# Loading the second expert matrix in whole rows, with the combine weights prepared among the experts' matmuls

## The chip, the cores and the metric

The kernel runs on one core of a Trainium2 chip. The metric is the device time of one execution in microseconds; the time of a kernel is the median of its runs.

## The reference

Three layers follow each other on 4,608 tokens (8 batches of 576) of width 512.

```python
# 1. attention in chunks of 64 tokens, 8 heads of 64
attn = softmax(q_c @ k_c.T / sqrt(64)); x = attn @ v_c
# 2. a feed-forward layer, 512 -> 2048 -> 512
h = np.maximum(x @ w_in, 0.0); x = h * h @ w_out
# 3. soft mixture of 8 experts with 4 slots each
logits = x @ phi                                  # 4608 x 32
slot_input = softmax(logits, over tokens).T @ x   # 32 x 512
for e in range(8):
    slot_out[e] = np.maximum(slot_input[e] @ w1[e], 0.0) @ w2[e]
out = softmax(logits, over slots) @ slot_out      # 4608 x 512
```

w1 is 8 x 512 x 1024 and w2 is 8 x 1024 x 512, all float32: 16.8 MB each. The output is 9.44 MB.

## The kernel before

The tokens go through in 36 tiles of 128 (64 tokens of two batches each), gathered in blocks of three. For most of the time TensorE makes the hidden layer of a block (`moe_h`, L727), turns it (L761) and keeps it in buffers G; w_out is never applied to tokens, only to slot sums. A running softmax over tokens (`soft(b)`) adds the block's G, weighted, to the slot sums (L928).

The last block is the one the change touches. Its `soft` runs a chain: logits Ls (L854), the sum over quarters (L864), their maximum (L874 to L876, nm), the exponential dts on ScalarE (ACT, L877), its transposes (L917), the weights dd (L919), 24 matmul pieces over G (L928), the sum acc on VectorE (DVE, L939). Then `slot_turn` transposes acc (L807), `slot_rows_of` multiplies by w_out (L817), each copied out by `halves` (L801 on ACT, L802 on DVE, both from one PSUM bank), and `slot_inputs` (L827, L831) makes the experts' input siT. Between these, `c_two` prepares combine weights for four groups of four tiles: transposes on TensorE (L1047), two ACT copies a group (L1055, L1060) and a GpSimd subtraction (L1061).

Then come the experts. Their weights arrive in 64 units of 512 KB, 32 of w1 and then 32 of w2. `load_units` sends a unit as soon as two halves of 512 columns are free, from a list `free` that `give` and `release` fill: attention buffers of the last tiles, the buffers of w_in (wi), the last G after L928, those of w_out (wo) after L817, and places of units that have been used. A unit in one buffer goes in one DMA (L985 for w1, L994 for w2), one in two half places in two (L988, L999). `kept_tags` names eight buffers that end as homes of combine weights cT or of the turned hidden layer hT; `give` sets the first `(C_CHAIN + 1) // 2` of them aside empty, the others hold a unit first. All DMAs go through SyncE (SP) in the order that a planner sets by a simulated time; TensorE's order is that of the source, and so is that of all engines in the early part of the kernel.

w1's matmuls (L1468) go by group of four experts (g), row block (kk) and half; then the hidden layer (L1441, L1442) is turned (`hidden_T`, L1451). w2's matmuls (L1584) run twice, for output columns 0 to 255 (ch = 0) and 256 to 511 (ch = 1); a unit of w2 is 512 rows by 256 columns. After each half, `slot_rows` and `slot_parts` (L1492, L1497 to L1501) make the slot outputs s4. The output of half 0 (`out_group`: matmuls L1553, copies L1555 on DVE and L1557 on ACT) runs among the matmuls of half 1, and so do the other five groups of combine weights (`c_group`); the output of half 1 runs at the end. An output group of four tiles is one DMA (L1568); a single tile at the border of two batch pairs goes as two DMAs of 64 partitions by 1 KB (L1574, 16 in all).

## Time and profile before

| | us |
|---|---|
| median of 3 runs | 772.77 |
| lowest to highest run | 772.29 to 775.29 |
| the profiled execution, device time | 774.87 |
| its span on the core | 773.1 |

| engine | busy us | share of the span |
|---|---|---|
| PE (TensorE matmul) | 711.1 | 92% |
| ACT (ScalarE) | 457.3 | 59% |
| DVE (VectorE) | 428.1 | 55% |
| POOL (GpSimd) | 161.9 | 21% |

The span is the stretch between the first and the last instruction of the profiled execution; the device time holds a little more. A share of busy time is a mean over stages with different limits, so the rows below look at the last 100 us by themselves. In a window's row stand its length, the busy time of PE, PEld (weight loads), DVE, ACT and POOL with their counts of instructions, the granted TensorE clock (1.00 is 2.4 GHz), the mean busy share of the 16 DMA engines (it can read over 1) and the bytes that they moved per second. Matmuls in float32 show as two pieces each.

### The profile page before, as it was taken

Reading aid. Unit: us, or ns where it says so; the run is one execution under the profiler, and the core shown is the slowest. Engines: PE = TensorE matmul, PEld = TensorE weight load, DVE = VectorE, ACT = ScalarE, POOL = GpSimd, SP = SyncE. Lnnn points to the kernel's source line nnn. Section 1 sums busy time; section 2 is a strip of 40 time slices with the busy share of each in tenths; the row PEclk is TensorE's granted clock in tenths of the full one; section 3 lists DMA queues with packets and bytes.
Section 4 is the critical chain, followed back from the end, with each engine's and each line's share of the span. In section 5 each row is a group of like instructions: output and inputs, shape, how many; then the busy total and the mean of one; then the engine's idle time right before and its main releaser. Section 6 shows DMA issues by size and latency. Waiting matters only on the chain.

```text
span 773.1 us, 16704 instructions
## 1 busy us (share of the span) xinstructions
PE 711.1 (92%) x6612; PEld 457.7 (59%) x6612; DVE 428.1 (55%) x908; ACT 457.3 (59%) x951; POOL 161.9 (21%) x209
## 2 busy tenths in 40 slices
PE   5788999898999999999999999999999999969790
PEld 3677776665666566565665656666666565524350
DVE  4789996267756656567665566566656201012160
ACT  3668787664656666666676566566766555531150
POOL 3222221131222312223132231322223100030000
PEclk9799999999999999999999999999999999999995
DMA  7897933233455534455544655454556523759998
GB/s 158 215 257 180 218 123 124 72 66 83 98 117 103 103 76 97 91 103 104 101 97 83 103 101 112 75 103 89 99 88 171 159 69 112 277 178 354 347 355 255
DMA packets 242589, 110.47 MB, mean 143 GB/s; under 512 B 201808, under 2 KB 235600, under 8 KB 242512
## 3 DMA queue, kind: packets, MB, share of 16 engines
q1 hardware_dynamic: 242512, 109.41, 57.7%
q8 instruction: 52, 0.85, 0.5%
q14 instruction: 25, 0.20, 0.1%
HBM read 78.71 MB, written 9.44 MB: 114 GB/s over the span
## 4 chain that ended last, share of the span: by engine, by line
PE 71%; DMA 10%; DVE 9%; ACT 4%; issue 1%; POOL 1%; SPq 1%; DVEq 0%; POOLq 0%; ACTq 0%
PE hps L727 41%; PE gT L761 7%; PE misc L928 4%; PE L L778 4%; DMA unit<-in_moe_w_dram 3%; PE ehps L1468 2%; DVE qk L276 2%; DMA qkT<-qk 2%; DMA qkv<-in_k_dram 2%; DMA qkv<-in_q_dram 1%; PE misc L332 1%; DMA qkv<-in_v_dram 1%; DVE stage L281 1%; PE misc L498 1%; DVE qk L275 1%
## 5 line engine op out<-in xcount | busy, mean ns | idle before, releaser
L727 PE MATMUL hps<-xb,wi 128*128 128x384 f16 (+2 forms) x2400 | 409.2, 321 | 0.3
L727 PEld LDWEIGHTS <-wi 128*128 128x128 f16 x2400 | 225.1, 98 | 139.9 <-issue 18.3
L742 ACT ACTIVATE g<-hps,inv_w 128x384 f32<-128x384 f32 (+1 forms) x200 | 112.6, 563 | 113.0 <-PE hps L727 110.8
L182 DVE TENSOR_REDUCE am<-qkv 128x1 bf16<-128x512 f32 x90 | 61.9, 687 | 89.9 <-DMA qkv<-in_v_dram 45.8
L188 ACT ACTIVATE G<-gT 128x384 f32<-128x384 f32 (+1 forms) x200 | 94.1, 471 | 17.9 <-PE gT L761 15.3
L761 PE MATMUL gT<-ident,g 128*128 128x128 f32 x576 | 98.3, 278 | 4.6 <-ACT G L188 3.7
L749 ACT ACTIVATE g<-g 128x384 f32<-128x384 f32 (+2 forms) x188 | 96.9, 515 | 1.5
L761 PEld LDWEIGHTS gT<-ident,g 128*128 128x128 f32 x576 | 73.0, 144 | 29.6 <-ACT g L749 7.1
L420 POOL TENSOR_SCALAR vbd<-qkv,as 64x512 f16<-64x512 f32 x54 | 37.2, 689 | 87.5 <-PE misc L500 71.8
L471 POOL TENSOR_TENSOR ex<-ex,rs 128x512 f32<-128x512 f32 x27 | 29.3, 1083 | 122.4 <-DVE rs L468 110.3
L410 DVE SCALAR_TENSOR_TENSOR qk<-qkv,as,qk 128x512 f16<-128x512 f32 x54 | 39.7, 762 | 20.4 <-ACT qk L405 19.8
L425 DVE SCALAR_TENSOR_TENSOR vbd<-qkv,as,vbd 64x512 f16<-64x512 f32 x54 | 44.7, 828 | 0.7
L778 PE MATMUL L<-g,wp 128*32 128x384 f32 x384 | 41.7, 498 | 0.0
L405 ACT ACTIVATE qk<-qkv,as 128x512 f16<-128x512 f32 x54 | 36.8, 717 | 7.9 <-DVE as L215 7.9
L484 POOL TENSOR_TENSOR p<-ex,p 128x512 f16<-128x512 f32 x27 | 36.2, 1341 | 16.5 <-ACT p L481 15.9
L481 ACT ACTIVATE p<-ex 128x512 f16<-128x512 f32 x27 | 17.0, 629 | 34.6 <-POOL ex L471 34.4
L928 PE MATMUL misc<-G,dd 128*32 128x512 f32 x288 | 35.1, 622 | 0.5 <-DVE rs__8963 L936 0.5
L435 DVE COPY qbd<-qkT 64x1024 f16<-64x1024 f16 x54 | 23.3, 431 | 18.3 <-DMA qkT<-qk 17.5
L510 DVE SCALAR_TENSOR_TENSOR xb<-misc,xb 128x512 f16<-128x512 f32 x27 | 18.5, 685 | 26.5 <-ACT xb L504 26.2
L223 POOL TENSOR_SCALAR iv_all<-ai 128x1 f32<-128x1 f32 x27 | 7.4, 273 | 108.5 <-DVE ai L218 107.6
L854 DVE TENSOR_TENSOR Ls<-L,iv_all 128x384 f32<-128x384 f32 x12 | 6.7, 557 | 41.5 <-PE L L778 41.5
L461 ACT ACTIVATE ex<-ex,es 128x512 f32<-128x512 f32 x27 | 19.4, 718 | 17.0 <-DVE ex L455 16.9
(156 smaller groups left out, 1018.9 us busy)
## 6 DMA issues: line engine op xcount, KB each, us to landing
unit<-in_moe_w_dram SPq DMA_DIRECT2D x34, 512.0 KB, 4.5
unit<-in_moe_w_dram SPq DMA_DIRECT2D x60, 256.0 KB, 5.9
qkv<-in_q_dram SPq DMA_DIRECT2D x72, 128.0 KB, 3.3
qkv<-in_k_dram SPq DMA_DIRECT2D x72, 128.0 KB, 3.5
qkv<-in_v_dram SPq DMA_DIRECT2D x72, 128.0 KB, 3.3
stage<-in_moe_w_in_dram SPq DMA_DIRECT2D x16, 512.0 KB, 5.3
stage<-in_moe_w_out_dram SPq DMA_DIRECT2D x16, 512.0 KB, 5.8
out_dram<-o SPq DMA_DIRECT2D x14, 512.0 KB, 6.3
```

What stands on the lines that cost most here:

```text
L182: dve.tensor_reduce(out=am, in_=src, axis=AX.X, op=ALU.max, apply_absolute_value=True)
L188: act.activation(out=out, in_=in_, func=ACTF.Copy)
L405: act.activation(out=qk16[:, 2 * a], in_=flat[:, a], func=ACTF.Copy, scale=v["s"][:, a : a + 1])
L410: dve.scalar_tensor_tensor(out=qk16[:, 2 * a + 1], in0=flat[:, a], scalar=v["s"][:, a : a + 1], in1=qk16[:, 2 * a], op0=ALU.mult, op1=ALU. ...
L420: pool.tensor_scalar(out=dst[0], in0=vin, scalar1=v["s"][pr, 2:3], scalar2=1.0, op0=ALU.mult, op1=ALU.mult,)
L425: dve.scalar_tensor_tensor(out=dst[1], in0=vin, scalar=v["s"][pr, 2:3], in1=dst[0], op0=ALU.mult, op1=ALU.subtract,)
L727: pe.matmul(hp, wi[f][:, wl, kt], xb[:, xl, kt], start=(nm == 0), stop=(nm == 3 * KT - 1))
L742: act.activation(out=g, in_=hp, func=ACTF.Relu, scale=sc)
L749: act.activation(out=g, in_=g, func=ACTF.Square)
L761: pe.transpose(gt_ps[b, f][:, j], g[:, j * P : (j + 1) * P], ident)
L778: pe.matmul(L_ps[g0][NS * x : NS * x + NS, :n], wp[:, QF * q + x], g[:, x, :n], start=(q == 0), stop=(q == NQ - 1), tile_position=(0, NS * x),
L928: pe.matmul(y[NS * g : NS * g + NS], dd[:, j], G_q[b, g][:, j], start=(j == 0), stop=(j == n - 1), tile_position=(0, NS * g), skip_group_c ...
```

## The change

- **C_CHAIN** goes from 4 to 0. `c_two` then does nothing in the last block's chain, and no kept buffer is set aside empty, so the first two hold a unit each. All nine groups of combine weights go through `c_group`: three among w1's matmuls (the condition on C_EARLY, unchanged, now holds), six among w2's.
- **`slot_turn` and `slot_rows_of`** work in two column halves, each in a PSUM bank of its own; ACT copies the first, DVE the second. The matmuls of `slot_rows_of` become twice as many with half the columns.
- **From the last block on**, ACT and DVE too run in source order.
- **w2 in whole rows**: 20 of its 32 units ("rows": experts 0 to 3 whole, g = 0, and the first quarter of experts 4 to 7, g = 1) hold 256 whole rows of one expert, two rows to a partition, 4 KB in one run (two runs of 2 KB where the home is split). Their matmuls serve both column halves at once, in two PSUM accumulators. The other 12 ("part") hold 128 rows of four experts in 256 columns, half 0 first, then half 1. `hidden_T` takes its columns with a stride of two to fit.
- **The output** is cut anew: groups of four tiles of the first two batch pairs by column halves (half 0 among and after the last matmuls, half 1 at the very end); between them pairs of tiles with all 512 columns, and the single tiles two by two, in four DMAs of 256 KB.

Of the last hunks of the diff only what is added and what stays is shown.

```diff
--- before.py
+++ after.py
@@ -31,7 +31,7 @@
-C_CHAIN = 4
+C_CHAIN = 0
...
@@ -796,30 +796,31 @@
         for r in (32, 96):
             dve.memset(second[r : r + 32], -1.0)
 
-    def halves(out, in_):
-        n = in_.shape[-1] // 2
-        act.activation(out=out[:, :n], in_=in_[:, :n], func=ACTF.Copy)
-        dve.tensor_copy(out[:, n:], in_[:, n:])
+    def half_out(h, out, in_):
+        copy(("act", "dve")[h], out[:, h * DM // 2 : (h + 1) * DM // 2], in_)
 
     def slot_turn():
-        ps = misc()
-        for c in range(QF):
-            pe.transpose(ps[:, c * P : (c + 1) * P], acc[:, c * P : (c + 1) * P], ident)
         fin["yz"] = yz = big.tile([P, 2, DM], F32, tag="g1", name="yz")
-        yT = yz[:, 0]
-        halves(yT, ps)
+        for h in range(2):
+            ps = misc()[:, : DM // 2]
+            for x in range(QF // 2):
+                c = h * QF // 2 + x
+                pe.transpose(ps[:, x * P : (x + 1) * P], acc[:, c * P : (c + 1) * P], ident)
+            half_out(h, yz[:, 0], ps)
 
     def slot_rows_of():
-        ps = misc()
         yT = fin["yz"][:, 0].rearrange("p (c g s) -> p c g s", c=QF, s=NS)
-        for c in range(QF):
-            for g in range(NQ):
-                pe.matmul(
-                    ps[NS * g : NS * g + NS], yT[:, c, g], wo[QF * g + c],
-                    start=(c == 0), stop=(c == QF - 1), tile_position=(0, NS * g),
-                    skip_group_check=True,
-                )
-        halves(fin["yz"][:, 1], ps)
+        for h in range(2):
+            ps = misc()[:, : DM // 2]
+            for c in range(QF):
+                for g in range(NQ):
+                    pe.matmul(
+                        ps[NS * g : NS * g + NS], yT[:, c, g],
+                        wo[QF * g + c][:, h * DM // 2 : (h + 1) * DM // 2],
+                        start=(c == 0), stop=(c == QF - 1), tile_position=(0, NS * g),
+                        skip_group_check=True,
+                    )
+            half_out(h, fin["yz"][:, 1], ps)
 
     def slot_inputs():
         sip = misc()
@@ -849,6 +850,10 @@
     def soft(b):
         s0, n = blocks[NB if b == 1 else b]
         last = s0 + n == NT
+        if last:
+            ctx.enter_context(
+                tc.manual_schedule(engines={mybir.EngineType.Activation, mybir.EngineType.DVE})
+            )
         L, iv = L_ps.pop(b), iv2_all[:, s0 : s0 + n]
         Ls = big.tile([P, 4, P], F32, tag="Ls", name="Ls")[:, :n]
         dve.tensor_tensor(
@@ -955,12 +960,17 @@
...
 
     DH = DM // NCH
-    RT = 1024 // DH
-    units = [(0, 0, 4 * g + e, kk) for g in range(2) for kk in range(KT) for e in range(4)]
+    SPLIT = FT // 4
+    units = [("w1", 4 * g + e, kk) for g in range(2) for kk in range(KT) for e in range(4)]
     units += [
-        (1, ch, 4 * g + e, kk)
-        for ch in range(NCH) for g in range(2) for kk in range(FT // RT) for e in range(4)
+        ("rows", 4 * g + e, m)
+        for g in range(2) for m in range((SPLIT if g else FT) // 2) for e in range(4)
     ]
+    units += [("part", ch, ft) for ch in range(NCH) for ft in range(SPLIT, FT)]
+    def w2_rows(e, m):
+        return w2[e, 2 * P * m : 2 * P * (m + 1)].rearrange("(p t) d -> p t d", t=2)
 
     out_tags = (f"qkv{NT % 2}", f"qkv{(NT - 1) % 2}", f"G{idle_G[0]}")
     kept_tags = [f"{x}{y % 2}" for y in (NT - 1, NT) for x in ("qk16", "qkT", "qbd", "vbd")]
@@ -975,30 +985,28 @@
...
             home[u] = (a, b)
+            if u[0] == "w1":
+                _, e, kk = u
+                src = w1[e, kk * P : (kk + 1) * P, :].rearrange("p (h d) -> p h d", h=2)
+            elif u[0] == "rows":
+                src = w2_rows(*u[1:])
             else:
+                _, ch, ft = u
+                m = ft // 2
+                src = w2[4:, 2 * P * m : 2 * P * (m + 1), ch * DH : (ch + 1) * DH].rearrange(
+                    "e (p t) d -> p t e d", t=2
+                )[:, ft % 2]
+            n = src.shape[1] // 2
+            if whole_home:
+                to = a[0][:, a[1] : a[1] + 1024].rearrange("p (t d) -> p t d", t=2 * n)
+                sp.dma_start(out=to, in_=src)
+            else:
+                for h, (t, o, _) in enumerate((a, b)):
+                    to = t[:, o : o + 512].rearrange("p (t d) -> p t d", t=n)
+                    sp.dma_start(out=to, in_=src[:, h * n : (h + 1) * n])
 
     def freed(pool_, tag, n):
         t = pool_.tile([P, n], F32, tag=tag, name="unit", **({} if pool_ is big else {"bufs": 1}))
@@ -1447,8 +1455,9 @@
         for h in range(2):
             htp = ps2.tile([P, FT // 2, P], F32, tag=f"ht{h}", name="htp")
             for ft in range(FT // 2):
-                f0 = (h * FT // 2 + ft) * P
-                pe.transpose(htp[:, ft], hs[:, f0 : f0 + P], ident)
+                m, t = divmod(h * FT // 2 + ft, 2)
+                rows = hs[:, 2 * P * m : 2 * P * (m + 1)].rearrange("p (x t) -> p t x", t=2)
...
@@ -1505,114 +1514,119 @@
...
+    def out_buffer():
+        tags = [t for _, _, t in free]
+        for tag in tags:
+            if not todo and 512 * tags.count(tag) == size_of[tag] >= 1024:
+                free[:] = [x for x in free if x[2] != tag]
+                break
+        else:
+            tag = out_ring.pop(0)
+        out_ring.append(tag)
+        return big.tile([P, 1024], F32, tag=tag, name="o")
+    out_ring = list(out_tags)
+    banks = ("eh00", "eh01", "eh10", "eh11", "ht0")
+    bank = [0]
+    by_batch = out.rearrange("(b s) d -> s b d", s=S)
+    def out_group(parts, chs):
+        n, w = len(parts), len(chs) * DH
+        flat = out_buffer()
+        items = [(i, c, ch) for i, c in parts for ch in chs]
+        for x0 in range(0, len(items), 2):
+            ops = ps2.tile([P, 2, DH], F32, tag=banks[bank[0] % 5], name="ops")
+            for x, (i, c, ch) in enumerate(items[x0 : x0 + 2]):
+                rows = cT[i // 8][:, i % 8 + (c or 0)]
+                pe.matmul(ops[:, x], rows, s4_h[ch], start=True, stop=True)
+            dst = flat[:, x0 * DH : (x0 + 2) * DH].rearrange("p (x d) -> p x d", x=2)
+            if bank[0] % 2:
+                dve.tensor_copy(dst, ops)
+            else:
+                act.activation(out=dst, in_=ops, func=ACTF.Copy)
+            bank[0] += 1
+        o = flat[:, : n * w].rearrange("p (t d) -> p t d", t=n)
+        cols = slice(chs[0] * DH, chs[0] * DH + w)
+        bp, ci = divmod(parts[0][0], CPB)
+        if parts[0][1] is not None:
+            r0 = (2 * bp + parts[0][1]) * S + ci * CH
+            sp.dma_start(
+                out=out[r0 : r0 + n * P, cols].rearrange("(t p) d -> p t d", p=P), in_=o
+            )
+        else:
+            s0, (bq, cj) = ci * CH, divmod(parts[-1][0], CPB)
+            assert n == 2 and ci == cj
+            for c in range(2):
+                to = by_batch[s0 : s0 + CH, 2 * bp + c : 2 * bq + c + 1 : 2 * (bq - bp), cols]
+                sp.dma_start(out=to, in_=o[CH * c : CH * c + CH])
+    both = tuple(range(NCH))
+    quads, pairs, lone = [], [], []
     for bp in range(NT // CPB):
+        tiles_of = range(bp * CPB, (bp + 1) * CPB)
+        even = [i for i in tiles_of if i % 2 == 0 and in_pairs(i)]
+        lone += [(i, None) for i in tiles_of if not in_pairs(i)]
         for c in range(2):
+            rows = [(i, c) for i in even]
+            if bp < 2:
+                quads.append(rows)
             else:
+                pairs += [rows[x : x + 2] for x in range(0, len(rows), 2)]
+    lone.sort(key=lambda x: x[0] % CPB)
+    pairs[1:1] = [lone[x : x + 2] for x in range(0, len(lone), 2)]
+    sops = [ps2.tile([P, DH], F32, tag=f"so{ch}", name="sop") for ch in range(NCH)]
+    def rows_times(g, ft, ch, rows):
+        for ei in range(4):
+            pe.matmul(
+                sops[ch][32 * ei : 32 * ei + 32], hT_g[g][:, ft, 32 * ei : 32 * ei + 32], rows(ei),
+                start=(g == 0 and ft == 0), stop=(g == 1 and ft == FT - 1),
+                tile_position=(0, 32 * ei), skip_group_check=True,
+            )
+    for g in range(2):
+        for ft in range(SPLIT if g else FT):
+            m, t = divmod(ft, 2)
+            for ch in range(NCH):
+                rows_times(
+                    g, ft, ch,
+                    lambda ei: part_of(("rows", 4 * g + ei, m), t)[:, ch * DH : (ch + 1) * DH],
                 )
+            if t:
                 for ei in range(4):
+                    release(("rows", 4 * g + ei, m), 0)
+                    release(("rows", 4 * g + ei, m), 1)
                 load_units()
+            if waiting and ft == 1:
                 hidden_T(*waiting.pop())
+            if c_todo and (t or g):
+                c_group(c_bank(f"ht{ft % 2}" if 1 in hT_g else "ht1"))
+    def last_rows(ch, ft):
+        u = ("part", ch, ft)
+        rows_times(1, ft, ch, lambda ei: part_of(u, ei // 2)[:, ei % 2 * DH : (ei % 2 + 1) * DH])
+        release(u, 0)
+        release(u, 1)
+    for ft in range(SPLIT, FT):
+        last_rows(0, ft)
+    slot_parts(0, slot_rows(0, sops[0]))
+    firsts = [quads[0][:2], quads[0][2:], *quads[1:]]
+    for ft in range(SPLIT, FT):
+        if FT - ft < len(firsts):
+            out_group(firsts.pop(0), (0,))
+        last_rows(1, ft)
+    so_sb = slot_rows(1, sops[1])
+    out_group(firsts.pop(0), (0,))
+    slot_parts(1, so_sb)
+    assert not firsts
+    for rows in pairs:
+        out_group(rows, both)
+    for rows in quads:
+        out_group(rows, (1,))
```

## Rows read from the trace of the kernel before

**Rows 1.** The page's 40 slices of the span: granted clock and DMA, in tenths

```profile
PEclk9799999999999999999999999999999999999995
DMA  7897933233455534455544655454556523759998
```

**Rows 2.** Windows of 2 us: busy time by engine, granted clock, DMA share, GB/s

```profile
678.00:680.00 2.00, 0.21 (x3) 0.21 (x3) 0.04 (x1) 1.87 (x5) 2.00 (x2) 1.00 0.02 6
...
682.00:684.00 2.00, 2.00 (x12) 0.44 (x8) 0.00 (x0) 0.00 (x0) 0.00 (x0) 0.50 0.00 0
```

**Rows 3.** Waits of SP's queue, 672 to 700 us: total, times, longest

```profile
SPq L985 <- PE misc L928: 12.1, 1, 12.1
```

**Rows 4.** Windows of 4 us behind the two runs of 64 KB outputs

```profile
752.00:756.00 4.00, 1.66 (x12) 1.33 (x11) 2.66 (x5) 2.06 (x4) 0.00 (x0) 1.00 0.62 187
768.00:772.00 4.00, 0.00 (x0) 0.00 (x0) 0.00 (x0) 0.00 (x0) 0.00 (x0) 0.50 0.53 126
```

**Rows 5.** DMA packets of 688:692, 696:704 (loads), 744:751 and 757:768 us (outputs)

```profile
DMA packets 431, 1.56 MB, mean 391 GB/s; under 512 B 46, under 2 KB 46, under 8 KB 431
...
DMA packets 2798, 2.80 MB, mean 350 GB/s; under 512 B 81, under 2 KB 2797, under 8 KB 2797
...
DMA packets 2714, 2.70 MB, mean 385 GB/s; under 512 B 80, under 2 KB 2714, under 8 KB 2714
...
DMA packets 3742, 3.71 MB, mean 337 GB/s; under 512 B 120, under 2 KB 3742, under 8 KB 3742
```

**Rows 6.** The chain of waits, 640 us to the end: start, length, what

```profile
651.17 2.71 PE misc L928 x24
...
675.22 0.91 PE misc L864 x2
...
676.61 0.60 ACT cT L1055
...
679.07 0.67 ACT dts L877 x2
...
680.69 4.46 PE misc L928 x24
...
688.25 0.39 ACT yz L801
...
688.68 3.76 PE misc L817 x32
...
694.45 3.64 PE ehps L1468 x32
...
704.16 1.02 PE htp L1451 x8
...
738.24 0.59 PE cps L1047 x4
```

**Rows 7.** Timeline of the last block's chain: start, length, instruction [idle before, releaser]

```profile
673.21 0.55 PE L761 MATMUL gT<-ident,g 128*128 128x128 f32 x3 [0.81 <-ACT g L749]
...
676.96 0.15 DVE L876 TENSOR_SCALAR nm<-rm 128x1 f32<-128x1 f32 x1
...
686.09 0.66 PE L807 MATMUL misc<-ident,acc 128*128 128x128 f32 x4
```

**Rows 8.** Timeline of w2 and the output

```profile
712.29 5.25 PE L1584 MATMUL sop<-unit,hT 128*32 128x256 f32 x86
...
742.27 0.14 PEld L1584 LDWEIGHTS sop<-unit,hT 128*32 128x32 f32 x2 [0.50 <-DMA unit<-in_moe_w_dram]
...
746.29 0.38 ACT L1492 ACTIVATE so_sb<-sop 128x256 f32<-128x256 f32 x1 [1.09 <-PE sop L1584]
...
748.41 5.25 PE L1553 MATMUL ops<-s,cT 128*128 128x256 f32 x36 [0.99 <-DVE s L1501]
...
749.19 5.47 DVE L1555 COPY o<-ops 128x512 f32<-128x512 f32 x9 [0.83 <-DMA out_dram<-o]
...
763.61 7.11 SPq L1574 DMA_DIRECT2D out_dram<-o  x8
```

112 lines of the change are left out of this document (5 added, 107 removed).

## Prediction

> **What bounds the kernel now.** I read the page's forty slices first: TensorE (PE) is full almost to the end, but the last slices are DMA's: the DMA line stands at 9 or more from 690 us on [rows 1]. So the last 100 us are a stage of their own, and the changed code lies in it alone; before it the kernel is TensorE's and nothing there is touched. The windows of 2 us split this stage in two. Until 685 us the loads stand still, moving 6 and then 0 GB/s [rows 2]; the queue's own waits say why: SP held one load for 12.1 us until the matmuls of L928 let go of their buffers [rows 3]. From there it is a race of bytes: the last units of w1, the 32 units of w2 (512 KB each) and 9.44 MB of output. Two places of that race are not full: 752 to 756 us and 768 to 772 us [rows 4].
>
> So what counts is when the transfers start again, how many bytes are left, how fast they go, and where the queue runs dry.
>
> **The change, part by part.** All against the profiled execution: span 773.1 us, device time 774.87, the 1.8 us around the span unchanged. The median, 772.77, is 2.1 us less; I take the sum off the median.
>
> *Two buffers hold weights.* With C_CHAIN = 0 `give` no longer sets two 1,024-column buffers aside, so two more units load early, in a stretch in which the DMA engines had room: they stood at 0.02 and 0.00 [rows 2]. That is 1.05 MB less afterwards, at 391 GB/s [rows 5]: **-2.7 us** (nothing, if they only fill the time in which the queue now waits, to -2.7).
>
> *No combine weights in the chain.* `c_two(0)` queued four ACT copies ahead of the softmax's exponential: the first starts at 676.61 and the exponential (dts) only at 679.07, though its input nm is done at 677.11 [rows 6, 7]. Gone, dts starts at 677.13: 1.94 us. The 24 matmul pieces of L928 behind it took 4.46 us here and 2.71 in the block before [rows 6]; the granted clock, 1.00 before, stands at 0.50 (1.2 instead of 2.4 GHz) in the middle of them [rows 2], after TensorE had lain idle from about 677 until dts was done near 679.7, 2.8 us. Now the gap runs from 676.1, where L864 ends, to 677.8: 1.7 us. After one of 0.81 at 673.2 [rows 7] the clock held. 1.7 lies a little nearer to that, so I take -1.25 (0 to -1.75). L928 frees the G buffers, so the loads start **3.2 us** earlier (1.9 to 3.7). The wo buffers, whose release now waits for the second half of the column split (about 0.8 us later within its step), come well inside the 8 us that six units in the G buffers keep the queue busy.
>
> *Two halves in slot_turn and slot_rows_of.* ACT's yz stood behind four more copies of `c_two(1)`, until 688.25 [rows 6], though the transposes begin at 686.09 and take 0.66 [rows 7]; with them gone and each half in its own bank, the first yz starts near 686.5, both are done at 687.0, and L817 begins there instead of at 688.68: 1.65 us sooner. The doubled number of matmuls has half the columns: 64 pieces of 256 columns at 5.25/86 = 0.061 us [rows 8] are 3.9 us against 3.76 [rows 6], so nothing. With the 3.2 us, w1's matmuls begin at 694.45 - 4.85 = 689.6. This is TensorE's, not DMA's, and worth nothing by itself; it pays for the next point.
>
> *Combine weights of three groups among w1's matmuls, six among w2's.* Each group is 0.6 us of TensorE (cps [rows 6]), a Pool copy, an ACT copy and a DVE subtraction, all beside the loads. TensorE: w1 is 128 pieces at 3.64/32 [rows 6], 14.6 us, plus tp and htp at 1.0 each [rows 6], three groups 1.9 and half a us of waiting for banks: done at 708.6. The rows of w2, 160 pieces at 0.061, with htp 1.0, six groups 3.6 and 0.7 of waiting: 15.1, done at 723.7. The cover is that the loads are later still (below); if it is gone, each us costs one.
>
> *Whole rows of w2.* 20 of 32 units now come in runs of 2 or 4 KB instead of 1 KB. In 688 to 692, packets of 2 KB and more move 391 GB/s; in 696 to 704, packets of 1 KB move 350 [rows 5]. 10.49 MB: 30.0 us become 26.8, **-3.1 us** (0 to -3.4). The other 12 units stay at 1 KB, but with twice the distance between runs: no such row here; I take 350, bounds 337 and 391 [rows 5], +0.7 and -1.9. The stride of two in the transposes of hs has no row: nothing, bounds 0 and one more htp each, 2 us on TensorE, inside its cover. The Trainium skill (DMA: Bandwidth & Descriptors, Specifications) speaks against this term: from 512 B on a transfer is at line rate, and HBM gives a core about 358 GB/s, so longer runs would bring nothing. Here 391 and 385 GB/s stand above that figure [rows 5].
>
> *Outputs.* The single tiles at the pair borders go out in 16 DMAs of 64 KB, which SP issues at 7.11/8 = 0.9 us each [rows 8], too slow to keep the engines busy. Behind the first eight the rate falls to 187 GB/s over 4 us [rows 4]; 0.75 MB that need 2.1 us at a rate between 337 and 385 [rows 5]: -1.9. The second eight are the kernel's end: 126 GB/s over 4 us [rows 4], 0.5 MB that need 1.5 us at 337; -2.5, less 0.6 that I leave for any last transfer: -1.9. They become four DMAs of 256 KB, away from the end. Together **-3.8 us** (-2 to -4.4). 5.2 MB go out in 2 KB runs instead of 1 KB; the same 1 KB form shows 385 and 337 [rows 5], so I take nothing, bounds 1.9 either way.
>
> *The new junction.* Only 2.1 MB of output (the first columns of the groups of four) are ready before w2 is through; 9.44 less 2.1 MB wait for it. w2's last wait for a load ends at 742.27 [rows 8]; less 9.0 (2.7 + 3.2 + 3.1) it is 733.3, so column half 0 is complete six units (9 us at 350) earlier, at 724.3, after TensorE's 723.7. Then so_sb to ops 2.1 us [rows 8], and the first output goes to the queue near 729.5, four us before the loads end. After them the 2.1 MB last until 739; the second slot chain starts at 734 and its first copies end at 737.9. I allow **+1 us** (0 to +2). Copies keep up: nine on DVE in 5.47 us, as many on ACT beside them [rows 8], are 4.7 MB, which the queue needs 12 us for. ACT and DVE in source order: behind a waiting so_sb (ACT) stand only output copies that come later anyway.
>
> *Sum:* -2.7 - 3.2 - 3.1 - 3.8 + 1.0 = -11.8. Span 761.3, median **761.0**. Best ends together -15.8 (757).
>
> **The rivals.**
> *Rows bring nothing.* 350 GB/s is what HBM gives whenever the queue is long, and the 391 is a short burst. For: 696 to 704 is steady, 688 to 692 short. Against: 385 over 7 us of output in 744 to 751 [rows 5]. Without 3.1: 764.1. By the rule of the Trainium skill named above this is the outcome.
> *The queue runs dry between weights and outputs.* TensorE may reach column half 0 late: its cover is under 1 us, and a group's chain (Pool, TensorE, ACT, DVE, now in source order) can stall it at each of nine places. A full stall at each, 0.6 us on ACT [rows 6] and 0.6 on DVE [rows 8], is 11 us, less the 4 us of queued work: +7, so 768. For: no output can fill the gap. Against: six units in flight and copies that fit between two steps.
> *Slower:* the clock. If w1 and w2 run at 0.50, as L928 did [rows 2, 6], pieces take 4.46/2.71 = 1.65 times: w1 24 us, the rows 16, the rest a few us more; half 0 is done near 740, its first output near 746 and the buffers come late too; with the group stalls of the last rival about 20 us of dry queue eat the gain: 778. It decides where half 0 is over 12 us late. For: TensorE waits on loads here. Against: late in w2 it waited on loads too, and the page's clock line has nothing under 9 there [rows 1].
> *It doesn't do what it says:* the early units and the earlier release only move the wait, the queue being filled from other buffers: without 2.7 and 3.2, 766.9. Against: the engines stood at nothing from 678 to 684 [rows 2].
> *More:* clock kept and outputs at 385 throughout: 757.
>
> **How the numbers follow.** Forecast 761.0: 0.58. Rows nothing (764.1): 0.14. No early start (766.9): 0.05. Dry queue (768, spread 765 to 773): 0.12, half of it within 0.5%. Slower: 0.06. More (757): 0.05. 0.5% is 3.9 us, about what a measurement of this kernel tells from no change. Faster: 0.58 + 0.14 + 0.05 + 0.06 + 0.05, less 0.02 from the edges, 0.86; same 0.08; slower 0.06. The range reaches to the dry queue's middle and stops short of the best: 757.5 to 768.5.
>
> **What would show it.** In the changed profile: dts right behind nm; L928's last run under 3.5 us; the loads starting again near 682; windows near 390 GB/s while rows load and near 350 after; the last wait of sop for a load near 733; no window under 300 GB/s between 690 and the last 2 us. Wrong if: rows go at 350; an empty window stands between the last load and the first pair's output; a wait of sop for ACT or DVE in place of loads; or L928 is still at 0.50.

## The result and the profile after

| | before | changed |
|---|---|---|
| median, us | 772.53 | 761.07 |
| lowest to highest of 4 runs | 772.03 to 775.29 | 758.60 to 762.14 |
| the profiled execution, device time | 774.87 | 762.14 |
| its span | 773.1 | 760.3 |

The ratio is 0.9843, with a 95% interval of 0.9815 to 0.9870: 11.5 us less by the medians, against 761.0 forecast and a range of 757.5 to 768.5.

Before the result is taken apart, one thing about the spans. The first line below is of the chain of waits of the kernel before, the other of the changed one (start, length, what): the instruction with which the last block's chain begins.

```profile
674.61 0.57 DVE Ls L854
...
672.29 0.57 DVE Ls L859
```

Ahead of it every engine has the same instructions in the same order in both kernels, except that SP sends two more loads near 600 us. Yet it starts 2.3 us sooner here, and over the fourteen executions that were profiled for this study it starts anywhere from 670.4 to 676.3 us. The two loads are not the reason: the second Ls of the execution, long before them, already starts at 190.2 us before and at 187.5 here. So 2.3 of the 12.8 us between the two spans are no work of the change. From here on I count the **stage**: from the start of Ls to the end of the span. It took 98.5 us before and 88.0 after: **10.5 us**.

The changed kernel's slices of the page (granted clock in tenths, DMA share in tenths), which answer to [rows 1]:

```profile
PEclk9899999999999999999999999999999999999996
DMA  8898834234545455434645455545546832659999
```

DMA is full in the last four slices, from 684 us on, and the clock stays up until the last. Next, the chain of waits of the changed kernel, which answers to [rows 6 and 8]:

```profile
672.90 0.93 PE misc L869 x2
...
674.64 0.16 DVE nm L881
674.83 0.68 ACT dts L882 x2
...
676.29 4.58 PE misc L933 x24
...
682.67 3.78 PE misc L817 x64
...
688.04 3.64 PE ehps L1477 x32
...
725.51 6.51 DMA unit<-in_moe_w_dram
732.07 0.64 PE sop L1584 x8
...
733.38 0.61 PE s4p L1506 x2
...
734.96 0.64 PE ops L1543 x3
```

The exponential dts now stands right behind its input nm. The 24 pieces on the G buffers (L933, which was L928) still take 4.58 us, as in [rows 6]. Behind them the loads restart. That is seen in the timeline of SP's queue (start, time for four issues), the first line before, the second after:

```profile
685.16 1.75 SPq L985 DMA_DIRECT2D unit<-in_moe_w_dram  x4
...
680.76 1.75 SPq L1004 DMA_DIRECT2D unit<-in_moe_w_dram  x4
```

From Ls that is 10.55 us before and 8.47 after. I call this moment the **second start**; from it to the end the stage took 87.9 us before and 79.5 after.

Windows of the changed kernel (columns as in [rows 2 and 4]; the last is GB/s):

```profile
676.00:678.00 2.00, 1.73 (x12) 0.50 (x16) 0.68 (x4) 0.00 (x0) 0.00 (x0) 0.72 0.00 0
678.00:680.00 2.00, 2.00 (x14) 0.43 (x8) 0.00 (x0) 0.00 (x0) 0.00 (x0) 0.50 0.00 0
...
730.00:736.00 6.00, 5.07 (x39) 3.37 (x39) 2.94 (x5) 3.14 (x7) 0.00 (x0) 1.00 0.96 324
736.00:744.00 8.00, 7.08 (x49) 6.19 (x47) 8.00 (x14) 7.46 (x13) 0.00 (x0) 1.00 0.94 287
744.00:752.00 8.00, 0.00 (x0) 0.00 (x0) 0.08 (x1) 0.00 (x0) 0.00 (x0) 0.57 1.02 387
```

The clock falls to 0.50 in the middle of L933, as it did before [rows 2]. The two holes of [rows 4] are gone, but the output has a dent of its own: 287 GB/s over 8 us. DMA packets of the changed kernel in 702:708 (whole rows), 716:728 (the last 12 units, 1 KB), 744:751 (pairs of tiles, 2 KB) and 754:758 us (groups of four, 1 KB):

```profile
DMA packets 1267, 2.32 MB, mean 387 GB/s; under 512 B 141, under 2 KB 141, under 8 KB 1266
...
DMA packets 4280, 4.17 MB, mean 348 GB/s; under 512 B 237, under 2 KB 4278, under 8 KB 4278
...
DMA packets 1409, 2.71 MB, mean 388 GB/s; under 512 B 84, under 2 KB 84, under 8 KB 1409
...
DMA packets 1380, 1.37 MB, mean 344 GB/s; under 512 B 38, under 2 KB 1380, under 8 KB 1380
```

Packets of 2 KB and more move at 387 or 388, loads and outputs alike; those of 1 KB at 348 and 344. The last two rows are two forms of output a few us apart. For outputs that does not yet make the length of the run the cause: in the kernel before, outputs in 1 KB runs moved 385 GB/s in one stretch and 337 in another [rows 5].

### The profile page after: what moved, and what is told of

It is laid out like the page before. It is cut to its first block, busy times and chain, and to the rows that moved or that the text cites. A ratio compares the mean times of both kernels' runs of the same rounds, so it can differ in the third digit from the quotient of the medians.

```text
span 760.3 us, 16721 instructions
## 1 busy us (share of the span) xinstructions
PE 704.4 (93%) x6644; PEld 455.8 (60%) x6644; DVE 430.2 (57%) x912; ACT 455.0 (60%) x947; POOL 157.2 (21%) x205
## 4 chain that ended last, share of the span: by engine, by line
PE 72%; DVE 10%; DMA 10%; ACT 2%; POOL 1%; issue 1%; SPq 1%; DVEq 0%; POOLq 0%; ACTq 0%
PE hps L727 42%; PE gT L761 7%; PE L L778 4%; PE misc L933 4%; DMA qkT<-qk 2%; PE ehps L1477 2%; DMA unit<-in_moe_w_dram 2%; DVE qk L276 2%; DMA qkv<-in_k_dram 1%; DMA qkv<-in_v_dram 1%; PE sop L1584 1%; DMA pT<-p 1%; DVE o L1546 1%; PE misc L498 1%; DVE qk L275 1%
## 5 line engine op out<-in xcount | busy, mean ns | idle before, releaser
L933 PE MATMUL misc<-G,dd 128*32 128x512 f32 x288 | 35.1, 622 | 0.4 <-DVE rs__8934 L941 0.4
```

What stands on the lines that cost most here:

```text
L933: pe.matmul(y[NS * g : NS * g + NS], dd[:, j], G_q[b, g][:, j], start=(j == 0), stop=(j == n - 1), tile_position=(0, NS * g), skip_group_c ...
```

## The experiments

All are edits of the changed kernel. The times of their profiled executions, in us, counted from Ls (the last column: median device time and number of runs). The 24 pieces are the matmuls over the G buffers, L928 before and L933 in the changed kernel:

| kernel | 24 pieces, start to end | second start | second start to end | stage | device |
|---|---|---|---|---|---|
| before | 6.06 to 10.54 | 10.55 | 87.92 | 98.47 | 772.53 (4) |
| changed | 3.98 to 8.46 | 8.47 | 79.51 | 87.98 | 761.07 (4) |
| e1_hold | 3.98 to 8.46 | 8.47 | 82.85 | 91.32 | 765.19 (8) |
| e3_run1k | 3.98 to 8.20 | 8.22 | 83.61 | 91.83 | 766.00 (10) |
| e2_chain | 3.98 to 6.76 | 6.78 | 82.84 | 89.62 | 763.83 (6) |
| e8_planner | 4.13 to 9.48 | 9.49 | 79.35 | 88.84 | 764.24 (2) |
| e4_fill | 3.98 to 6.76 | 6.78 | 79.78 | 86.56 | 761.38 (4) |
| e13_bank | 3.98 to 6.76 | 6.77 | 79.07 | 85.84 | 762.15 (2) |
| e7_pework | 3.98 to 6.76 | 6.77 | 82.86 | 89.63 | 765.94 (2) |
| e10_early | 3.98 to 6.76 | 6.77 | 81.05 | 87.82 | 760.37 (6) |
| e5_lone_late | 3.98 to 6.76 | 6.77 | 79.36 | 86.13 | 763.53 (2) |
| e9_lone_small | 3.98 to 6.76 | 6.77 | 81.01 | 87.78 | 763.80 (2) |
| e11_halfparts | 3.98 to 8.46 | 8.47 | 84.47 | 92.94 | 765.78 (2) |
| e12_best | 3.98 to 6.76 | 6.77 | 80.53 | 87.30 | 761.33 (6) |

Kernels with the same code behind the second start (changed, e4_fill) differ by 0.3 us in the fourth column, so differences under about 0.5 us are not read there. The medians come from five sets of runs, in which the kernel before had medians from 772.27 to 775.33, so 3 us between two lines of the last column can lie in the sets.

**The bytes.** *e1_hold* sets the first two kept buffers aside empty again, and nothing else.

```diff
-            if tag in kept_tags[: (C_CHAIN + 1) // 2]:
+            if tag in kept_tags[:2]:
```

> The changed kernel, with only the first two kept buffers set aside empty again (no weights in them); the chain stays as changed. The stage from the last block's Ls to the end of the span is 98.5 us before and 88.0 after. My theory (the stage is a race of bytes): 1.05 MB more have to come after the loads start again, at about 390 GB/s, so the last load lands 2.7 us later and the stage takes 90.7 us; device time +2.7. Rival (the early units only fill time in which the queue would wait anyway, or the late outputs set the end): 88.0, no change.

The same second start, and the end 3.34 us later. Its last wait of w2 for a load ends here (chain of waits):

```profile
734.89 0.64 PE sop L1584 x8
```

That is 54.5 us behind the second start, against 51.3 in the changed kernel (732.07 above). Two units more (1.05 MB) behind the second start reach the end in full, and somewhat more than that: at 391 GB/s they would be 2.7. Where the other 0.6 us come from isn't shown. Ratio to before 0.9904 (0.9871 to 0.9936), against 0.9843.

*e3_run1k* loads each unit of whole rows in two DMAs that move 1 KB runs, with homes, matmuls and order kept.

```diff
-        return w2[e, 2 * P * m : 2 * P * (m + 1)].rearrange("(p t) d -> p t d", t=2)
+        return w2[e, 2 * P * m : 2 * P * (m + 1)].rearrange("(p t) (h d) -> p h t d", t=2, h=2)
...
+            if u[0] == "rows":
+                for h, (t, o, _) in enumerate((a, b)):
+                    to = t[:, o : o + 512].rearrange("p (t d) -> p t d", t=2)
+                    sp.dma_start(out=to, in_=src[:, h])
+                continue
...
-                    lambda ei: part_of(("rows", 4 * g + ei, m), t)[:, ch * DH : (ch + 1) * DH],
+                    lambda ei: part_of(("rows", 4 * g + ei, m), ch)[:, t * DH : (t + 1) * DH],
```

> The changed kernel with the whole-row units of w2 still two rows to a partition and in the same order, but each fetched as two transfers of one column half: runs of 1 KB instead of 2 or 4 KB. Same bytes, same matmuls. My theory (long runs go at 385 to 415 GB/s, runs of 1 KB at 350): the 10.5 MB need 30.0 us instead of 26, the last load lands 3 to 4 us later and the stage is 91 to 92 us. Rival (350 GB/s is only what the memory gave at that time, as the Trainium skill, DMA: Bandwidth & Descriptors, Specifications, has it with full rate from 512 B on and about 358 GB/s from HBM for a core): rate and stage as in the changed kernel, 88.0.

DMA packets of the changed kernel in 692:708, and of e3_run1k in 692:716 us:

```profile
DMA packets 2530, 6.42 MB, mean 401 GB/s; under 512 B 279, under 2 KB 279, under 8 KB 2529
...
DMA packets 8577, 8.29 MB, mean 345 GB/s; under 512 B 504, under 2 KB 8575, under 8 KB 8575
```

401 against 345 GB/s, steady over 16 and 24 us, and 4.1 us from the second start to the end. The edit also makes two DMAs of each unit that lay in one place, but that is not the reason: in the changed kernel most loads of 702:708 (387 GB/s) and of 716:728 (348 GB/s) came in DMAs of 256 KB too, the first in 2 KB runs and the second in 1 KB runs. So for these loads the length of the run is worth it, and the rival in which rows bring nothing is out. By the Trainium skill (DMA: Bandwidth & Descriptors, Specifications) 512 B are enough for line rate and HBM gives a core about 358 GB/s (a share that the same page, under Bandwidth, gives for two cores streaming; this kernel runs on one). Here 1 KB is not enough for these loads, and 401 stands above that figure. The measurement decides.

**The chain.** *e2_chain* prepares four groups in the chain again (C_CHAIN = 4), ACT and DVE still in source order.

```diff
-C_CHAIN = 0
+C_CHAIN = 4
```

> The changed kernel with C_CHAIN = 4: four groups of combine weights are prepared in the chain to the experts again, and two buffers are set aside for them; rows, outputs and source order stay as changed. My theory: the 2.7 us of the two units and 1.9 us for the exponential that stands behind four copies on ACT again, so the loads start again about 10.4 us after Ls instead of 8.5, and the stage is 88.0 + 4.6 = 92.6 us. Rival (the clock of the 24 matmul pieces behind the exponential matters too and is better or worse with the transposes in the gap): their run of 4.5 us changes by more than 0.3. Rival (the outputs set the end): 88 to 89.5.

*e8_planner* does the opposite: no groups in the chain, but ACT and DVE in the planner's order.

```diff
-        if last:
-            ctx.enter_context(
-                tc.manual_schedule(engines={mybir.EngineType.Activation, mybir.EngineType.DVE})
-            )
```

> The changed kernel with ACT and DVE left to the planner's order in the last block and behind it. In the run with C_CHAIN = 4 and source order the exponential stood right behind its maximum although the four copies were there, so the 1.9 us may belong to the source order as much as to the missing copies. Theory A (either edit alone takes the copies away from in front of the exponential): with no copies in the chain the planner's order costs nothing there, dts 3.0 us after Ls, stage 88.0. Theory B (the planner puts something else ahead): dts later than 3.0 us after Ls, or waits of TensorE for ACT and DVE in w2's rows, stage over 89.

From the chains of waits of e2_chain (first three lines) and of e8_planner (the other three), then a window of e8_planner:

```profile
672.60 0.57 DVE Ls L859
675.14 0.03 ACT dts L882
675.99 0.49 ACT cT L1063
...
673.52 0.57 DVE Ls L855
676.05 0.68 ACT dts L878 x2
677.67 5.45 PE misc L929 x24
...
676.00:678.00 2.00, 0.87 (x7) 0.59 (x11) 0.83 (x6) 0.85 (x3) 0.00 (x0) 0.55 0.04 14
```

dts stands 2.54 us behind Ls in e2_chain and 2.53 in e8_planner, as in the changed kernel (2.54); before it was 4.46. The four copies stood ahead of the exponential because the planner had put them there. In source order they run behind it (cT at 675.99). So either edit by itself takes the 1.92 us away. The expectation for e2_chain (92.6) failed on this and on the clock: its 24 pieces took 2.8 us, as its rival allowed. In e8_planner the second start comes 1.0 us later than in the changed kernel all the same, because the granted clock had fallen before the pieces began (0.55 over the window above) and they took 5.45 us. e2_chain as a whole is slower than the changed kernel from the second start on (82.84): it also sets the two buffers aside, and that part agrees with e1_hold's 82.85. From the medians neither edit can be priced more finely.

**The clock.** *e4_fill* puts 16 transposes that nobody reads into the gap in which TensorE waits for dts.

```diff
+        if last:
+            warm = ps_h.tile([P, 512], F32, tag="h", name="warm")
+            for x in range(FILL):
+                pe.transpose(warm[:, x % 4 * P : (x % 4 + 1) * P], ident, ident)
```

> The changed kernel with 16 transposes of the identity into a spare PSUM bank, put behind the matmul of the sum over quarters, so that TensorE is busy while DVE and ACT make the maximum and the exponential of the last block. Nothing reads them. My theory on the missed term: the granted clock falls because TensorE idles ahead of the 24 pieces, which take 4.48 us at 0.50 and 2.71 at 1.00. With the gap filled they take 2.7 to 3.0, the loads start 1.5 to 1.8 us sooner and the stage is 86.3. Rival (the clock falls for another reason, the few columns of these pieces say, or the idle time around acc): 4.48 us again and 88.0.

The first line is from the timeline of the changed kernel (idle time before in brackets), the second from the chain of e4_fill, the next two from the timeline and the chain of e5_lone_late, whose chain is that of the changed kernel, with no fill. Then a window of e5_lone_late with its pieces in it, and the pieces of e3_run1k:

```profile
675.55 0.37 PE L922 MATMUL misc<-ident,dts 32*128 32x32 f32 x3 [1.74 <-ACT dts L882]
...
674.49 2.89 PE misc L938 x24
...
677.99 0.37 PE L922 MATMUL misc<-ident,dts 32*128 32x32 f32 x3 [1.74 <-ACT dts L882]
678.72 2.89 PE misc L933 x24
...
680.00:682.00 2.00, 1.49 (x16) 0.26 (x8) 0.36 (x1) 0.00 (x0) 0.00 (x0) 1.00 0.00 0
...
676.76 4.33 PE misc L933 x24
```

With the gap filled the pieces take 2.9 us instead of 4.6, the second start is 1.7 sooner, and the stage 1.4 shorter. The medians don't show it (761.38 against 761.07), and e5_lone_late has the same idle 1.74 us and kept the clock too. Over the executions with that gap it was lost in five (changed, e1_hold, e3_run1k, e8_planner, e11_halfparts) and kept in three (e5, e7, e9). Where the gap was filled (e4, e10, e12, e13) or shortened to 0.86 by transposes of combine weights (e2_chain) it was kept in five of five. That leans to the fill, but a split of that kind comes up by chance some 4 to 8 times in 100 (counted from these thirteen): it isn't settled. The outcome is not fixed by the code: up to here the changed kernel and e5_lone_late have the same instructions. And where the clock fell, it did not fall at one place: the pieces took 4.33 us (e3_run1k), 4.58 (changed, e1_hold, e11_halfparts) or 5.45 (e8_planner), against 2.89 where it held, so the second start came 1.4 to 2.7 us later. The Trainium skill (TensorE: Matmul & The Clock Gate, Part 1: The HAM clock gate) says of a kernel's start that the point at which the clock turns varies between runs. At the very start it stands at 1.00 in all fourteen executions here. The traces show the like later: from 17 to 21 us of the span, in code that all the kernels share, it stood at 0.50 in three executions (before, e2_chain, e7_pework) and at 1.00 in the others, and in the middle of the kernel, after this gap, it is five against three.

**Halves and banks.** *e13_bank* is e4_fill with `slot_turn` and `slot_rows_of` of the kernel before, one bank for both copies.

```diff
+    def halves(out, in_):
+        n = in_.shape[-1] // 2
+        act.activation(out=out[:, :n], in_=in_[:, :n], func=ACTF.Copy)
+        dve.tensor_copy(out[:, n:], in_[:, n:])
...
+        for c in range(QF):
+            for g in range(NQ):
+                pe.matmul(
+                    ps[NS * g : NS * g + NS], yT[:, c, g], wo[QF * g + c],
+                    start=(c == 0), stop=(c == QF - 1), tile_position=(0, NS * g),
+                    skip_group_check=True,
+                )
+        halves(fin["yz"][:, 1], ps)
```

> The changed kernel with the 16 transposes in the gap, and with slot_turn and slot_rows_of as before the change: one PSUM bank for both halves, ACT and then DVE copying from it. The changed version let w1's matmuls start 7.3 us after the loads' second start. By my prediction the split moves TensorE alone and is worth nothing by itself while TensorE is ahead of the loads: w1 starts 0.8 to 1.2 us later, the first output at most as much later, stage 86.6 as in e4_fill, or 0.3 more. Rival (the wo buffers set the loads: with whole columns they come free sooner, so the loads run earlier): last load up to 0.8 us sooner. Rival (TensorE is the bound of the rows): stage 87.5 to 88. If the fill holds the clock the 24 pieces take 2.8 us here too.

From the second start to w1's first matmul it is 9.3 us before, 7.3 in the changed kernel and in e4_fill, 7.9 here. So 0.6 of the 2.0 us come from the split and 1.4 from the copies that are gone: with no copies but the planner's order (e8_planner) it is 7.3 too, with the copies in source order (e2_chain) 8.6. The end does not get them: e13_bank is 0.7 shorter from the second start on than e4_fill. The last load lands 51.1 us behind the second start here and 51.5 in e4_fill, which would fit the later release of the wo buffers by the split; at this size it is a hint only.

**TensorE's cover.** *e7_pework* adds four unread transposes, 0.59 us, behind each of the ten row steps of w2: 5.9 us.

```diff
+            more = ps2.tile([P, 512], F32, tag="eh00", name="more")
+            for x in range(MORE):
+                pe.transpose(more[:, x % 4 * P : (x % 4 + 1) * P], ident, ident)
```

> The changed kernel with four transposes of the identity behind each of the ten row steps of w2, 0.59 us each time by the row of the same transposes, 5.9 us of TensorE in all; nothing reads them. My prediction put TensorE 0.6 us ahead of the loads at the end of the rows, so by it 5.3 us would show: last load unchanged, first output 5 us later, stage 88.0 + 5.3 less the 1 us of queue that was thin anyway = 92. The trace of the changed kernel shows TensorE done with the rows at 719.1 and the last load of column half 0 at 723.2, a cover of about 4 us: by it the stage is 89.5 to 90.

From the timelines: SP's first output issues in the changed kernel and in e7_pework, then the matmuls of the changed kernel that end the rows of w2 and half 0:

```profile
727.94 8.80 SPq L1555 DMA_DIRECT2D out_dram<-o  x6
...
734.96 7.43 SPq L1556 DMA_DIRECT2D out_dram<-o  x6
...
720.92 2.96 PE L1584 MATMUL sop<-unit,hT 128*32 128x256 f32 x48
```

Behind the second start the first output comes at 47.2 us in the changed kernel and at 51.9 here: 4.7 of the 5.9 us show, 1.2 were covered. The end is 3.35 later. So TensorE was some 1.2 us away from being the bound; in the kernels with the same loads and no added work the first output came at 47.0 to 47.6, so this is good to about 0.4. That the stage, 89.6, is what the expectation worked out from a cover of 4 us is luck: 3.35 us showed where 1.5 to 2 were expected, and the clock, which held in this execution, took 1.7 off.

*e10_early* is e4_fill with half 0's output groups put earlier, one ahead of each of the first five row blocks of half 1 and none behind its last.

```diff
-        if FT - ft < len(firsts):
+        if firsts:
...
-    out_group(firsts.pop(0), (0,))
```

> The changed kernel with the 16 transposes in the gap (as in e4_fill) and with the five first output groups placed one step apart from the first matmuls of the last half of w2 on, two steps sooner than in the changed kernel. In the changed kernel the windows between the last loads and the first pairs show 273 to 350 GB/s, so the queue is thin there. Theory A (the queue is thin because the first outputs come late): the first output goes 1.3 us sooner, the queue is filled behind the loads, 1 to 1.5 us less from the loads' second start to the end than the 79.5 of the changed kernel; with the clock held (second start 6.8 us after Ls) the stage is 85 to 85.5, the device time about 758.5. Rival (the thin stretch is the chain of the second half, which nothing else covers): 79.5 from second start to end, stage 86.3.

Its windows, columns as above:

```profile
728.00:732.00 4.00, 3.44 (x39) 2.07 (x35) 1.60 (x3) 1.58 (x3) 0.00 (x0) 1.00 0.86 288
732.00:736.00 4.00, 3.13 (x23) 2.66 (x22) 2.59 (x5) 2.73 (x6) 0.00 (x0) 1.00 0.59 206
```

The thin place at the junction, 324 GB/s over 6 us in the changed kernel, does not go away but deepens to 206. The first output came hardly sooner, 47.3 us behind the second start against 47.5 in e4_fill, not the 1.3 us that was expected; and the first pair of the second half was issued 1.6 us later, for the outputs went ahead of that half's own matmuls. It gained nothing (81.05 from the second start, against 79.78).

**The outputs.** *e5_lone_late* moves the four single-tile transfers further back.

```diff
-    pairs[1:1] = [lone[x : x + 2] for x in range(0, len(lone), 2)]
+    pairs[6:6] = [lone[x : x + 2] for x in range(0, len(lone), 2)]
```

> The changed kernel with the two groups of single tiles (four transfers of 256 KB from 64 partitions each) sent after six pairs instead of after one, when a long queue stands ahead of them. In the changed kernel the windows from 736 to 744 us, in which these four go, show 261 to 298 GB/s against 385 to 398 behind. Theory A (a transfer that reads only 64 of the 128 partitions is itself slow, about 200 GB/s): the dent moves to the place of the four transfers, with the same depth, and the stage stays at 88.0. Theory B (the queue is thin just after the second half of w2 and the place does not matter to these transfers): no dent at their new place, and the old one is filled by pairs, so the stage is 86 to 86.5.

*e9_lone_small* leaves them in place and sends each as two of 128 KB.

```diff
-            for c in range(2):
-                to = by_batch[s0 : s0 + CH, 2 * bp + c : 2 * bq + c + 1 : 2 * (bq - bp), cols]
-                sp.dma_start(out=to, in_=o[CH * c : CH * c + CH])
+            for x, by in enumerate((bp, bq)):
+                for c in range(2):
+                    r0 = (2 * by + c) * S + s0
+                    sp.dma_start(out=out[r0 : r0 + CH, cols], in_=o[CH * c : CH * c + CH, x])
```

> The changed kernel with the single tiles sent one by one, each batch half for itself: eight transfers of 128 KB that go from the lower and the upper 64 partitions in turn, at the same place. Theory A (only half of the partitions at a time is what is slow): with twice as many changes between the halves the engines work on both at once for longer, and the windows 736 to 744 rise towards 340 GB/s; stage 86.5 to 87.5. Theory B (thin queue): eight small transfers instead of four fill the queue worse, stage 88 to 89.

*e11_halfparts* sends every pair of whole rows as two DMAs of 64 partitions, with the same runs and bytes.

```diff
+            if len(chs) == 1:
+                sp.dma_start(out=to, in_=o)
+            else:
+                for c in range(2):
+                    sp.dma_start(out=to[CH * c : CH * c + CH], in_=o[CH * c : CH * c + CH])
```

> The changed kernel with each of the eight whole-row pairs sent as two transfers of 64 partitions (256 KB each, like those of the single tiles) instead of one of 128 partitions. Same bytes, same places in memory, same order. Theory A (a transfer that reads only 64 partitions runs at some 200 to 280 GB/s): the 4.2 MB of pairs need 15 to 21 us instead of 11, so 4 to 8 us more from the loads' second start to the end than the 79.5 of the changed kernel. Theory B (the single tiles are slow for their two places in memory, 1.3 MB or more apart, or for the thin queue): no more than 1 us.

Windows of e5_lone_late (three), e9_lone_small and e11_halfparts, then the timeline of the single-tile issues on SP in the changed kernel and in e9_lone_small:

```profile
737.00:746.70 9.70, 7.06 (x49) 6.19 (x47) 8.05 (x14) 7.43 (x13) 0.00 (x0) 1.00 0.99 357
746.70:750.70 4.00, 0.00 (x0) 0.00 (x0) 0.00 (x0) 0.00 (x0) 0.00 (x0) 0.78 0.92 285
750.70:754.00 3.30, 0.00 (x0) 0.00 (x0) 0.00 (x0) 0.00 (x0) 0.00 (x0) 0.50 1.03 377
...
740.00:744.00 4.00, 3.40 (x24) 2.89 (x22) 4.00 (x8) 3.79 (x7) 0.00 (x0) 1.00 0.83 196
...
738.00:756.00 18.00, 3.61 (x25) 3.07 (x24) 4.61 (x8) 4.00 (x7) 0.00 (x0) 0.67 0.88 272
...
736.97 3.41 SPq L1563 DMA_DIRECT2D out_dram<-o  x4
...
737.16 5.13 SPq L1564 DMA_DIRECT2D out_dram<-o  x8
```

In e5 the dent moves with the transfers, to 746.7 (285 GB/s, between 357 and 377), and the total stays (79.36); its stage of 86.13 is the figure of theory B, but only because the clock held. In e11 the stretch of pairs and single tiles runs at 272 GB/s and the end is 5.0 us later: these transfers from 64 partitions are slower than those from 128 of the same runs. Their half size alone is hardly the reason, for the loads of 702:708 came in DMAs of 256 KB over 128 partitions at 387. It is partly in the packets themselves: 0.88 of the engines' time for 272 GB/s, where whole transfers took 1.02 for 387, is 1.23 times the engine time for a byte. In the rest of the time the engines are idle, while SP issued the twenty transfers from 734.90 to 753.75 us without a pause, 0.94 us each; no run separates the two. e9 halves the size at 0.64 us an issue, falls to 196, and costs 1.5: there the pace of SP's issues, 128 KB in 0.64 us, is the bound.

*e12_best* puts e4_fill, e5_lone_late and e9_lone_small together, their edits as above.

> The changed kernel with the 16 transposes in the gap and with the single tiles both late (after six pairs, with a long queue ahead) and one by one (eight transfers of 128 KB, lower and upper partitions in turn). The filled gap held the clock in the two runs that had it, the unfilled one lost it in five of eight; if the fill is what holds it, the 24 pieces take 2.8 us again. Halves in turn behind a long queue should lift the 255 to 290 GB/s of the single tiles to 340 or more: 0.5 to 1 us less from the loads' second start to the end than the 79.4 to 79.8 of the kernels with whole single-tile transfers, stage 85.5 to 86. Rival (SP's time to issue eight transfers, 0.6 us each, sets their rate wherever they stand): 81 from second start to end, as in e9_lone_small, stage 87.8.

87.3 us, no better than e4_fill alone (86.56), and 80.5 from the second start, near the 81 of the rival. No version beat the changed kernel by more than the runs can tell: e10_early's 760.37 and e4_fill's 761.38 are both on the changed kernel's 761.07.

## Why the prediction was right, and where it was not

**What bounds it** (right). Bytes added behind the second start, or slowed, came out at the end: 3.3 us for 2.7 us of bytes (e1_hold), 4.1 for 3 to 4 (e3_run1k). A detail of the reading was off: the DMA line stands at 9 from 696 us on, not from 690, and its last slice is 8 [rows 1].

**Two buffers hold weights** (-2.7 forecast; right, slightly small). Undone, 3.3 us.

**No combine weights in the chain** (right in size, too narrow in cause). dts came 1.92 us sooner against 1.94. But I put it on C_CHAIN alone; source order for ACT does the same (e2_chain, e8_planner).

**The clock term** (-1.25; the step that failed). I had placed 1.74 us "a little nearer" to a gap after which the clock held, and taken a value in between. But the clock either holds or falls, and in the profiled execution it fell: L933 at 4.58, clock 0.50, the sign that I had named for being wrong. The pieces gained nothing, so the second start came 2.08 us sooner, not 3.2. In three other executions with the same gap it held. What decides between them stays open.

**Slot halves** (1.65 sooner to w1 and worth nothing by itself; nearly right). 2.0, of which the split gives 0.6. That wo's later release "comes well inside" is in doubt by some 0.4 us (e13_bank).

**TensorE's cover.** The rows ended where I had them (half 0's matmuls begin 48.6 us behind Ls, forecast 49.1), but I set that end against half 0's last load and left out half 0's own 24 matmuls, 2.96 us. With them my figures would have left no cover at all; e7_pework shows some 1.2 us. So the rival of the dry queue was nearer than its chance of 0.12 said.

**Whole rows** (-3.1; right, slightly small). Undone, 3.9 to 4.1: rows ran at 387 to 401 GB/s, and the 1 KB units at 348, as taken. The stride in the transposes, which I had set at nothing, does have a price, within the bounds. The first line is of the kernel before, the other of the changed one, both from the timeline:

```profile
704.09 1.09 PE L1451 MATMUL htp<-ident,hs 128*128 128x128 f32 x8
...
699.57 1.22 PE L1460 MATMUL htp<-ident,hs 128*128 128x128 f32 x8
```

Their weight loads went from 140 to 209 ns in the median, and each htp from 1.09 to 1.22 or 1.23 us, on TensorE, beside the loads.

**Early units and rows together.** From the second start to w2's last wait for a load 57.11 us became 51.31: 5.8, as forecast. To the last load's landing 57.75 became 51.26, 6.5, for in the kernel before the last load landed 0.64 us behind that wait. Undone one at a time the two give 3.2 and 4.3 of it, 7.5 in all; where the missing 1 to 1.7 us lie stays open.

**Outputs and junction** (-2.8 together; near in sum, wrong in parts). From the end of w2's last wait for a load to the end it was 773.1 - 742.27 = 30.8 us [rows 8] and is 760.3 - 732.07 = 28.2: -2.6. The 16 small transfers at SP's pace are gone, as I said, though that pace is not 0.9 us: of each eight issues the first three, with the queue still full, took 1.0 to 1.4 us and the other five 0.54 to 0.60. But the four of 256 KB were taken to run at full rate, and the windows in which they go don't: 64 partitions each, 287 GB/s over 8 us, 2.1 us lost against 387. I had overlooked that they take half the partitions. What may have made up for it is the point that I had set at nothing: 5.2 MB in 2 KB runs at 388 instead of 344 would be 1.7 us. That is argued, not shown: outputs of 1 KB runs had 385 as well as 337 before [rows 5], and no run sends these outputs in 1 KB runs or puts the old order of outputs back. The junction is thin, 324 GB/s over 6 us, about 1 us as allowed; sending the first outputs earlier does not cure it (e10_early), and the second half's own chain (732.07 to 734.96 in the chain of waits above) is the likely cause, not tested. Together: 3.8 less for the holes, 1.7 less for the runs, 2.1 more for the dent, 1 more for the junction, -2.4 of the -2.6. The 3.8 are the forecast's own, so that they add up proves little.

**The sum.** 11.8 forecast, 10.5 in the stage (2.1 to the second start, 5.8 to w2's last wait, 2.6 behind it): of the 1.3 missing, 1.1 are the clock term and 0.2 the outputs. The "best ends together -15.8" under the range is no sum of the bounds as given: these make -14.2, or -18.0 with the two ends of 1.9. That the profiled time (762.1) and the median (761.07) came so near is partly luck: 2.3 us of the profiled gain lie in code that the change does not touch, and the medians' 11.5 carry the same kind of spread. The sign "no window under 300 GB/s" failed (287); dts and the rates stood as named. The last wait of sop (732.07 for "near 733") and the second start (680.8 for "near 682") seem to, but Ls came 2.3 us sooner here for no work of the change: counted from Ls both were about 1.1 us late, which is the clock again.

## What to carry to other kernels

Where a stage is a race of bytes, count the bytes behind the moment when the queue starts again and give each form of transfer its own rate from the trace: here 4 KB or 2 KB runs over all 128 partitions moved at 387 to 401 GB/s, loads in 1 KB runs at 345 to 350, outputs in 1 KB runs at 337 to 385, and stretches with transfers of 64 partitions at 272 to 287. Moving work out of a waiting chain pays only for the instructions that really stand ahead of the next step; look at the order in the timeline, for a different order may give the same. Compare profiled executions from the last point ahead of the change that both kernels share, not by their spans.

## What the runs showed of the hardware that I had not expected

- Stretches with transfers of 64 partitions ran at 272 (e11_halfparts) and 285 to 287 GB/s, against 387 for the same 2 KB runs from 128.
- The granted clock after one and the same idle gap of 1.74 us fell to 0.50 in five executions, not at the same place in all, and stayed at full speed in three.
- The same instructions of TensorE, ACT, DVE and Pool ahead of the last block's Ls ended between 670.4 and 676.3 us, a spread of 0.8% of the span, while from the second start on the same code repeated to 0.3 us (79.51 and 79.78).
- A transpose whose weight load reads its columns with a stride of two had weight loads of 209 ns instead of 140, and eight of them took 1.22 us instead of 1.09.
